# Attention scores of two heads in one product, over 128 rows with zeros beside the keys

## The chip, the core and the metric

The kernel runs on one core of a Trainium2 chip. The metric is device time in microseconds (us) of one execution; lower is better. The kernel before takes 1866.67 us, the median of 3 runs (1866.61 to 1867.35). The five engines of a core run their own lists of instructions in order and wait for each other by semaphores: TensorE (PE: products, with the weight loads shown apart as PEld), VectorE (DVE), ScalarE (ACT), GpSimd (POOL) and SyncE (SP, which here issues DMAs).

## The reference

Three layers follow each other: an attention with banded masks, a dense mixture of 8 experts, and a feed-forward layer with a squared ReLU. The change lies in the attention alone.

```python
# q, k, v: (4, 8, 576, 64) float32
scores = (1 / sqrt(64)) * q @ k.transpose(0, 1, 3, 2)
rel = pos[:, None] - pos[None, :]
mask_plain = (rel >= 0) & (rel < 32)                       # heads 0 to 3
mask_dil = (rel >= 0) & (rel < 128) & (rel % 4 == 0)       # heads 4 to 7
scores = where(masks, scores, -1e9)
attn = exp(scores - max(scores)); attn = attn / (sum(attn) + 1e-9)
x = (attn @ v), heads side by side: (2304, 512)
P = gate(x @ w_gate)                      # Sinkhorn: 8 rounds of row and column sums
y = sum over e of P[:, e] * (relu(x @ w1[e]) @ w2[e])      # w1: 8 x 512 x 1024
out = (relu(y @ w_in) ** 2) @ w_out                        # w_in: 512 x 2048
```

## The kernel before

**Staging.** The attention works first, in the first 85 us or so of the span. The experts and the last layer follow, in products of float32r operands split into a high and a low part; they fill the rest of the span and no line of them is touched.

**Groups and slots.** Queries are cut into blocks of 32 (`QB`). A block sees 64 keys (`KB`): its own 32 and the 32 before it. For the dilated heads the positions are sorted by their remainder by 4 outside the kernel, so that their mask is a band too. Six blocks (`GB`) of four heads make a group; 4 batches x 2 sorts of heads x 3 thirds of the sequence make 24 groups. The function `slot(i)` writes out by hand what each engine does in one step of the pipeline: the scores of group i (`att_scores`), the exponential and the norm of group i-1 (`softmax`), the product with the values of group i-4 (`att_pv`), the transposes of group i-3 (`att_tr`), and the copy of group i-5 to its place (`att_x`). `fill(i)` adds three products of the first expert in ten of the later slots, `gate(...)` the gate's products in a few, and `warm_up(4)` four products on zeros in slots 0 to 2. The order on each engine is that of the code.

**Scores (L439 to L464).** One product (L448) writes the masks of the whole group into a PSUM bank: its stationary operand `spread_q` (L89) repeats a 32 x 32 identity over four heads, its moving operand is a row of masks (0 or -1e30). Then 24 products (L452), one for each block and head, add the scores. The rows of the array are the 64 elements of a head: two heads lie one above the other, in rows 0 to 63 and 64 to 127, and two pairs of heads lie side by side in the tile. The four heads of a block write to four strips of 32 partitions. Each of these float32 products is two weight loads and two matmul instructions of 64 columns. VectorE takes the maximum (L462) and subtracts it (L463).

**Transposes and values.** Three transposes (L482) turn a group's weights; two ScalarE copies (L487) put their halves into `pts`, a tile with zeros in the other half. `att_pv` (L496) has 12 products, 128 rows x 64 columns of weights: the two blocks that one transpose holds are multiplied in one product, because the keys of each stand beside zeros.

**Loads.** `load_qk(i + 2)` and `load_v(i - 1)` are issued by SP in `feed(i)`. The queries and keys of a group are one DMA of 416 KB into one of three buffers (L426 and L427), which becomes free when the scores of the group three before it are done; the values are one of 384 KB (L434). Each DMA signals one of eight semaphores in turn (DMAHW0 to DMAHW7), and SP waits with a DMA until the one that used its semaphore last has landed.

**The start (L1079 to L1107).** Memsets clear the mask tile's unused rows and the zero halves. ScalarE loads the first masks, casts them (L437), and then asks for `ident`. SP asks for groups 0 and 1, a tile of weights (512 KB), group 2 and the other masks. Seven products on zeros (L1098) run on TensorE meanwhile.

Of the kernel before, what the change touches and what calls it, by code (L numbers as in the profile page):

```python
# [10 lines left out]
F32 = mybir.dt.float32  # L11
F32R = mybir.dt.float32r
# [17 lines left out]
KCOLS = QC + PAD  # L30
DIL = 4
KC = DM // 128
FB = 256
# [18 lines left out]
def tile_kernel(ctx: ExitStack, tc: tile.TileContext, a):  # L52
    nc = tc.nc
# [9 lines left out]
    xfp = att.enter_context(tc.tile_pool(name="xfp", bufs=1))  # L63
    qkv = att.enter_context(tc.tile_pool(name="qkv", bufs=2))
# [19 lines left out]
    every = slice(0, KC)  # L84

    ident = const.tile([128, 128], F32, name="ident")
    mask = xfp.tile([128, 4 * GB + 2, KB], F32R, name="mask")
    mask_raw = xfp.tile([QB, 4 * GB + 2, KB], F32, name="mask_raw")
    spread_q = mask[:, :2].rearrange("p g k -> p (g k)")  # L89
    p_zero = [xfp.tile([128, 2, GB // 2, 4, QB], F32, name=f"pts{k}") for k in range(2)]  # L90
    wg = xfp.tile([128, KC, 32], F32, name="wg")
    warm = xfp.tile([128, 128], F32, name="warm")

# [9 lines left out]
    bufs = {"s": 2, "xt": 2, "pt": 1, "mm": 3}  # L103
# [177 lines left out]
    def xb():  # L281
        return post[0].tile([128, 2 * T], F32, tag="xb", name="xb", bufs=2)
# [137 lines left out]
    NG = len(groups)  # L420
    q_t, k_t, v_t, e_t, pt_t, xt_t = {}, {}, {}, {}, {}, {}

    def load_qk(i):
        if i < NG:
            b, hg, m = groups[i]
            z = qkv.tile([128, 2 * (QC + KCOLS)], F32, tag="qk", name="qk", bufs=3)  # L426
            nc.sync.dma_start(z, a["qk"][b, hg, m])  # L427
            q_t[i], k_t[i] = (y.rearrange("p (r n) -> p r n", r=2) for y in (z[:, :2 * QC], z[:, 2 * QC:]))

    def load_v(i):  # L430
        if i < NG:
            b, hg, m = groups[i]
            v_t[i] = qkv.tile([128, GB // 2, 4 * D], F32, tag="v", name="v", bufs=4)
            nc.sync.dma_start(v_t[i], a["v"][b, hg, m])  # L434

    def round_mask(g0, g1):
        nc.scalar.copy(mask[:QB, g0:g1], mask_raw[:, g0:g1])  # L437

    def att_scores(i):  # L439
        _, hg, m = groups[i]  # L440
        qt, kt = q_t.pop(i), k_t.pop(i)
        ps = psum.tile([128, 512], F32, tag="s", name="s")[:, :GB * KB].rearrange("p (g k) -> p g k", g=GB)
        k = m + 1 if hg else 0
        if hg == 0 and m > 0:
            mk = mask[:, 4:5, :].to_broadcast([128, GB, KB])
        else:
            mk = mask[:, 2 + GB * k:2 + GB * k + GB, :]
        nc.tensor.matmul(ps, spread_q, mk, start=True, stop=False, skip_group_check=True)  # L448
# [28 lines left out]
    def att_tr(i):  # L477

        ex = e_t.pop(i).rearrange("p g k -> p (g k)")
        ps = bank("s" if i >= NG - 2 else "pt")[:, :GB * KB]  # L480
        for c in range(GB // 2):
            nc.tensor.transpose(ps[:, c * 128:(c + 1) * 128], ex[:, c * 128:(c + 1) * 128], ident)  # L482
        pt_t[i] = p_zero[i % 2]
        for half in range(2):
            keys = slice(KB * half, KB * half + KB)
            copy = nc.vector.tensor_copy if half and i >= NG - 3 else nc.scalar.copy
            copy(pt_t[i][keys, half].rearrange("p c h q -> p (c h q)"), ps[keys])  # L487

    def att_pv(i):
        vt, pt = v_t.pop(i), pt_t.pop(i)  # L490
        xt_t[i] = psum.tile([128, 512], F32, tag="xt", name="xt")[:, :2 * QC].rearrange("p (r w) -> p r w", r=2)
        halves = xt_t[i].rearrange("p r (h w) -> p r h w", h=2)
        for c in range(GB // 2):
            for head in range(4):
                pr, h = divmod(head, 2)
                nc.tensor.matmul(  # L496
                    halves[D * h:D * h + D, pr, :, c * QB:c * QB + QB],
                    vt[:, c, head * D:head * D + D],
                    pt[:, :, c, head],
                    start=True,  # L500
                    stop=True,
                )

    def att_parts(i):
# [6 lines left out]
        else:  # L511
            n, step = S // DIL, DIL
        parts, c = [], 0
# [564 lines left out]

    with tc.manual_schedule():  # L1079
        nc.vector.memset(warm, 0.0)  # L1080
        for eng, g in ((nc.vector, slice(0, GB + 2)), (nc.gpsimd, slice(GB + 2, None))):
            for rows in (slice(QB, 2 * QB), slice(2 * QB, 128)):
                eng.memset(mask[rows, g].bitcast(F32), 0.0)
# [10 lines left out]
        nc.sync.dma_start(mask_raw[:, GB + 2:], a["mask"][:, GB + 2:])  # L1094

        ps = psum.tile([128, 512], F32, tag="s", name="s")
        for k in range(NWARM):
# [8 lines left out]
        nc.vector.tensor_copy(wr, warm)  # L1106
        nc.vector.memset(xr.bitcast(F32), 0.0)  # L1107
        gates = []
        last_lo = [lambda: None]

# [77 lines left out]
        def feed(i):  # L1188
            if i:
                load_qk(i + 2)  # L1190
                load_v(i - 1)
            if parts:
                parts.pop(0)()
            if 1 <= i < 4:
                round_mask(GB * i + 2, GB * i + GB + 2)
# [187 lines left out]
        for i in range(len(steps) + 1):  # L1383
# [30 lines left out]
            if mixed(i - 1):  # L1414
                v = l2_mixed(i - 1)
# [39 lines left out]
            if i + 1 in first[1:]:  # L1455
                c = first[1:].index(i + 1)
# [11 lines left out]
            if i == TURN + 2:  # L1468
                y = two(xb()) + two(xb())
# [40 lines left out]
def _layout(x):  # L1510
    q, k, v = x["q"], x["k"], x["v"]

    def order(z):
        lo = z[:, :4]
        hi = z[:, 4:].reshape(B, 4, S // DIL, DIL, D).transpose(0, 1, 3, 2, 4).reshape(B, 4, S, D)
        return np.stack([lo, hi], axis=1)
# [1 line left out]
    qo, ko, vo = order(q), order(k), order(v)  # L1518

    def pairs(z):  # L1520
        return z.reshape(B, 2, 2, 2, S, D).transpose(0, 1, 3, 5, 2, 4)
# [4 lines left out]
    ks = np.stack([kz[..., m * QC:m * QC + KCOLS] for m in range(NM)], axis=2)  # L1526

    vp = np.concatenate([np.zeros((B, 2, 4, PAD, D), v.dtype), vo], axis=3)
    vt = np.stack([vp[:, :, :, j * QB:j * QB + KB] for j in range(NB)], axis=3)
    vt = vt.reshape(B, 2, 4, NM, 2, GB // 2, KB, D).transpose(0, 1, 3, 4, 6, 5, 2, 7)  # L1530
    vt = vt.reshape(B, 2, NM, 128, GB // 2, 4 * D)

    def first(w, n):
        return w.reshape(KC, 128, n, FC, 128).transpose(2, 1, 3, 0, 4).reshape(n, 128, KC * FB)
# [10 lines left out]
    def split_at(o):  # L1545
# [1 line left out]

    first_block, split, after_split = split_at(0), split_at(QB // 2), band & (kk >= QB // 2)
    masks = [
        z[3 * (k % 2) + k // 2]  # L1550
        for z in (
            [first_block] + [band] * 5,
            [first_block, band, band, band, split, after_split],
            [band, band, band, first_block, band, band],
            [band, split, after_split, band, band, band],
        )
        for k in range(GB)
    ]
    arrays = {
        "qk": np.concatenate([z.reshape(B, 2, NM, 128, -1) for z in (qs, ks)], axis=-1),  # L1560
        "v": vt,
        "w_gate": np.pad(x["moe_w_gate"].reshape(KC, 128, E).transpose(1, 0, 2), ((0, 0), (0, 0), (0, 32 - E))),
        "w1": w1,
# [1 line left out]
        "w_in": first(x["moe2_w_in"], NS2),  # L1565
        "w_out": second(x["moe2_w_out"], NS2),
        "mask": np.concatenate(
            [np.tile(np.eye(QB, dtype=np.float32), (1, 4)).reshape(QB, 2, KB)]
            + [np.where(m, 0.0, NEG).astype(np.float32)[:, None] for m in masks],
            axis=1,  # L1570
        ),
# [22 lines left out]
```

## Time and profile before

| | |
|---|---|
| median of 3 runs | 1866.67 us (1866.61 to 1867.35) |
| the profiled execution: its own time | 1866.62 us |
| its span | 1864.8 us |
| TensorE busy | 1852.2 us, 99% of the span |
| VectorE, ScalarE, GpSimd busy | 88%, 48%, 41% |
| DMA | 493.28 MB, 265 GB/s over the span |
[...]

The span runs from the first instruction to the last; 1.8 us of the own time lie around it. A matmul's busy time overlaps with that of the matmuls beside it in other strips of the array, so a busy share near 100% does not say that nothing could be shorter. "issue" as a releaser is time in which an engine waited for nothing that the profile shows.

### The profile page before, as it was taken

Reading aid. Unit: us, or ns where it says so; the run is one execution under the profiler, and the core shown is the slowest. Engines: PE = TensorE matmul, PEld = TensorE weight load, DVE = VectorE, ACT = ScalarE, POOL = GpSimd, SP = SyncE. Lnnn points to the kernel's source line nnn. Section 1 sums busy time; section 2 is a strip of 40 time slices with the busy share of each in tenths; the row PEclk is TensorE's granted clock in tenths of the full one; section 3 lists DMA queues with packets and bytes.
Section 4 is the critical chain, followed back from the end, with each engine's and each line's share of the span. In section 5 each row is a group of like instructions: output and inputs, shape, how many; then the busy total and the mean of one; then the engine's idle time right before and its main releaser. Section 6 shows DMA issues by size and latency. Waiting matters only on the chain.

```text
span 1864.8 us, 28269 instructions
## 1 busy us (share of the span) xinstructions
PE 1852.2 (99%) x10209; PEld 1541.8 (83%) x10209; DVE 1648.2 (88%) x2357; ACT 902.9 (48%) x1553; POOL 760.4 (41%) x650
## 2 busy tenths in 40 slices
PE   9999999999999999999999999999999999999999
PEld 7788888888888888888888888888888888888887
DVE  7788999999999999997799999999998879875775
ACT  6752444555554544543443444444343465653454
POOL 4532656556656555553323323232222443321321
PEclk9999999999999999999999999999999999999999
DMA  8785576667666665768887787777676798889562
GB/s 294 249 332 181 213 252 242 257 243 241 231 228 245 244 231 219 254 220 343 325 320 267 288 296 278 283 274 288 246 288 250 304 355 292 284 310 387 196 255 77
DMA packets 154684, 493.28 MB, mean 265 GB/s; under 512 B 16992, under 2 KB 20720, under 8 KB 154544
## 3 DMA queue, kind: packets, MB, share of 16 engines
q1 hardware_dynamic: 154208, 491.22, 71.7%
q8 instruction: 80, 1.31, 0.3%
q14 instruction: 60, 0.49, 0.1%
q10 hardware_dynamic: 336, 0.26, 0.1%
HBM read 282.67 MB, written 208.74 MB: 264 GB/s over the span
## 4 chain that ended last, share of the span: by engine, by line
PE 93%; DVE 4%; ACT 1%; issue 1%; POOL 0%; DMA 0%; SPq 0%; ACTq 0%; POOLq 0%; DVEq 0%
PE pt L646 17%; PE mm L1013 16%; PE s L1013 14%; PE s L646 11%; PE xt L646 11%; PE mm L904 10%; PE mm L840 5%; PE xt L1013 2%; PE mm L883 2%; DVE g L736 1%; PE xt L496 1%; PE s L452 1%; DVE acc L1024 1%; PE s L904 1%; PE mm L646 0%
## 5 line engine op out<-in xcount | busy, mean ns | idle before, releaser
L736 DVE TENSOR_TENSOR g<-r,g 128x512 fp32r<-128x512 f32 x268 | 306.3, 1155 | 37.0 <-ACT g L733 35.1
L766 POOL TENSOR_TENSOR r<-mix,r 128x512 f32<-128x512 f32 x67 | 87.4, 1304 | 568.8 <-DVE mix L754 494.3
L1013 PE MATMUL s<-g,mixh 128*128 128x512 f32 x670 | 207.2, 390 | 1.1 <-ACT mm L1035 0.4
L1013 PE MATMUL mm<-g,w2h 128*128 128x512 f32 x670 | 206.5, 390 | 0.7 <-ACT s L1035 0.7
L733 ACT CAST g<-r 128x512 fp32r<-128x512 f32 x268 | 166.0, 620 | 66.4 <-PE s L1013 34.3
L1024 DVE TENSOR_TENSOR acc<-mm,acc 128x512 f32<-128x512 f32 x266 | 180.5, 681 | 1.8 <-PE mm L1013 1.8
L1024 DVE TENSOR_TENSOR acc<-s,acc 128x512 f32<-128x512 f32 x260 | 171.9, 682 | 0.1
L736 DVE TENSOR_TENSOR g<-mix,g 128x512 fp32r<-128x512 f32 x201 | 158.7, 790 | 2.9 <-ACT g L733 2.9
L733 ACT CAST g<-mix 128x512 fp32r<-128x512 f32 x201 | 124.7, 621 | 72.2 <-DVE mix L754 45.1
L1013 PEld LDWEIGHTS s<-g,mixh 128*128 128x128 f32 x670 | 125.4, 188 | 29.3 <-ACT s L1035 1.7
L1013 PEld LDWEIGHTS mm<-g,w2h 128*128 128x128 f32 x670 | 125.6, 188 | 27.3 <-ACT s L1035 1.1
L250 POOL TENSOR_TENSOR raw<-raw 128x256 f32<-128x256 f32 x36 | 37.9, 1053 | 238.2 <-DVE w2l L178 214.5
L1013 PE MATMUL mm<-g,w2l 128*128 128x512 f32 x335 | 130.4, 389 | 0.0
L805 ACT COPY s<-pt 128x512 f32<-128x512 f32 x79 | 46.5, 588 | 165.3 <-PE pt L646 165.3
L764 POOL TENSOR_TENSOR mix<-mix,r 128x512 f32<-128x512 f32 x67 | 88.5, 1320 | 87.9 <-DVE g L736 87.9
L646 PE MATMUL xt<-x_hi,sumh 128*128 128x512 f32 x316 | 123.7, 391 | 0.1
L646 PE MATMUL s<-x_hi,blkh 128*128 128x512 f32 x316 | 123.5, 391 | 0.0
L646 PE MATMUL s<-x_lo,blkh 128*128 128x512 f32 x316 | 123.2, 390 | 0.0
L646 PE MATMUL pt<-x_hi,sumh 128*128 128x512 f32 x316 | 123.1, 390 | 0.0
L646 PE MATMUL xt<-x_lo,sumh 128*128 128x512 f32 x316 | 123.1, 390 | 0.0
L646 PE MATMUL xt<-x_hi,suml 128*128 128x512 f32 x316 | 123.1, 389 | 0.0
L646 PE MATMUL s<-x_hi,blkl 128*128 128x512 f32 x316 | 123.1, 389 | 0.0
(299 smaller groups left out, 5026.0 us busy)
## 6 DMA issues: line engine op xcount, KB each, us to landing
raw<-in_w SPq DMA_DIRECT2D x62, 512.0 KB, 4.2
w_blkh<-blkh SPq DMA_DIRECT2D x40, 512.0 KB, 5.1
w_blkl<-blkl SPq DMA_DIRECT2D x40, 512.0 KB, 5.9
w_sumh<-sumh SPq DMA_DIRECT2D x40, 512.0 KB, 6.2
w_suml<-suml SPq DMA_DIRECT2D x40, 512.0 KB, 4.7
w_w2h<-w2h SPq DMA_DIRECT2D x40, 512.0 KB, 5.6
w_w2l<-w2l SPq DMA_DIRECT2D x40, 512.0 KB, 5.7
blkh<-w_blkh SPq DMA_DIRECT2D x40, 512.0 KB, 3.8
```

The source lines that it names most:

```text
L250: tt(out=r[:, 1, 1], in0=r[:, 0, 1], in1=r[:, 1, 1], op=ALU.add)
L646: nc.tensor.matmul(ps, w[:, c], z[:, x, j], start=start and k == 0, stop=stop and k == 5, skip_group_check=True)
L733: after(k, lambda: nc.scalar.copy(b[:, 0], src))
L736: lambda: nc.vector.tensor_tensor(out=b[:, 1], in0=src, in1=b[:, 0].bitcast(F32), op=ALU.subtract),
L764: after(6 if i in (TURN, first[3]) else 4, lambda: nc.gpsimd.tensor_tensor(out=r3, in0=r3, in1=r5, op=ALU.subtract))
L766: sub = lambda o, x, y: nc.gpsimd.tensor_tensor(out=o, in0=x, in1=y, op=ALU.subtract)
L805: at_once(lambda: nc.scalar.copy(made["s2"], bank_b))
L840: nc.tensor.matmul(ps, w[:, c], z[:, kc], start=k == 0, stop=k == len(terms) - 1)
L883: nc.tensor.matmul(ps, wt, g, start=n == 0, stop=n == len(terms) - 1)
L904: nc.tensor.matmul(ps, g[:, c0 * 128:c0 * 128 + 128], wt[:, fc], start=k == 0 and not seeded, stop=k == 3 * FC - 1, skip_group_check=bool( ...
L1013: nc.tensor.matmul(ps, w[wt][:, c], block[n][:, g], start=start and k == 0, stop=stop and k == 2, skip_group_check=True)
L1024: nc.vector.tensor_tensor(out=o, in0=ps, in1=o, op=ALU.add)
```

## The change

A group's queries and keys come in two DMAs of 64 rows each (208 KB each) into one static tile `kq_all` with three places. In a place, keys stand twice: the first 448 columns hold keys in rows 0 to 63 and zeros below them, the last 448 hold zeros in rows 0 to 63 and keys below. Between them stand the 384 columns of queries, with one head in rows 0 to 63 and another in rows 64 to 127. One product has all 128 rows, 32 columns of queries and 128 moving columns, the 64 keys of the first head and the 64 of the second; 12 products make a group's scores. The four strips of partitions now hold two halves of the group's blocks by two pairs of heads. VectorE clears the zeros once, six memsets of 64 x 448 at the start. The values, the masks and the copies are laid out anew for this; a mask row is given once for two heads and repeated by the access pattern, and the stationary operand spreads two blocks' masks, so that the mask tile is 14 rows of 64 on 64 partitions, not 26 on 32. At the start ScalarE also issues the second half of group 0 and `ident` ahead of the mask's cast.

```diff
-            z = qkv.tile([128, 2 * (QC + KCOLS)], F32, tag="qk", name="qk", bufs=3)
-            nc.sync.dma_start(z, a["qk"][b, hg, m])
-            q_t[i], k_t[i] = (y.rearrange("p (r n) -> p r n", r=2) for y in (z[:, :2 * QC], z[:, 2 * QC:]))
+            z = kq_all[:, KQW * (i % 3):KQW * (i % 3) + 2 * (QW + KW)]
+            nc.sync.dma_start(z[:D, :KW + QW], a["kq"][b, hg, m, :D])
+            eng.dma_start(z[D:, KW:KQW], a["kq"][b, hg, m, D:])
+            k_t[i] = z.rearrange("p (h n) -> p h n", h=2)
+            q_t[i] = z[:, KW:KW + QW].rearrange("p (r n) -> p r n", r=2)
...
-        for g in range(GB):
-            for head in range(4):
-                pr, rows = head // 2, slice(D * (head % 2), D * (head % 2) + D)
+        for c in range(CB):
+            for quarter in range(4):
+                part, pr = divmod(quarter, 2)
+                n = QB * (CB * part + c)
                 nc.tensor.matmul(
-                    ps[QB * head:QB * head + QB, 2 * (g % 3) + g // 3, :],
-                    qt[rows, pr, g * QB:g * QB + QB],
-                    kt[rows, pr, g * QB:g * QB + KB],
+                    whole[QB * quarter:QB * quarter + QB, c],
+                    qt[:, pr, n:n + QB],
+                    kt[:, :, KCOLS * pr + n:KCOLS * pr + n + KB],
...
-        nc.scalar.dma_start(mask_raw[:, :GB + 2], a["mask"][:, :GB + 2])
-        round_mask(0, GB + 2)
+        nc.scalar.dma_start(mask_raw[:, :CB + 2], a["mask"][:, :CB + 2])
+        load_qk(0, nc.scalar)
         nc.scalar.dma_start(ident, a["ident"])
-        load_qk(0)
+        round_mask(0, CB + 2)
         load_qk(1)
...
+        for k in range(3):
+            z = kq_all[:, KQW * k:KQW * k + KQW]
+            nc.vector.memset(z[D:, :KW], 0.0)
+            nc.vector.memset(z[:D, KW + QW:], 0.0)
+            if k == 0:
+                nc.vector.tensor_copy(wr, warm)
+                nc.vector.memset(xr.bitcast(F32), 0.0)
```

On TensorE, in slots 6 and 7, the list of before reads as follows (`xt` is the product with the values, `pt` the transposes, `s` the bank of masks and scores; x24 counts products):

```order
L496 MATMUL xt<-pts_93,v 64x2x32 x12
L482 MATMUL pt<-ident,ms 128x128 x3
L448 MATMUL s<-mask 128x384
L452 MATMUL s<-qk 32x64 x24
L496 MATMUL xt<-pts_92,v 64x2x32 x12
L482 MATMUL pt<-ident,ms 128x128 x3
L448 MATMUL s<-mask 128x384
L452 MATMUL s<-qk 32x64 x24
```

The same place of the changed kernel, on TensorE:

```order
L506 MATMUL xt<-pts_93,v 64x2x32 x12
L492 MATMUL pt<-ident,ms 128x128 x3
L454 MATMUL s<-mask 128x384
L462 MATMUL s<-kq_all 32x128 x12
L506 MATMUL xt<-pts_92,v 64x2x32 x12
L492 MATMUL pt<-ident,ms 128x128 x3
L457 MATMUL s<-mask 128x384
L462 MATMUL s<-kq_all 32x128 x12
```

Nothing changes its place; a slot has 12 score products of 128 columns where it had 24 of 64, and the other products stay in number.

On SP, from the load of group 6 on, the list of before with its waits (PE is the wait for the buffer, DMAHW that for an earlier DMA on the same semaphore):

```order
L427 DMA qk<-in_qk 128x832 [waits DMAHW7_49,DMAHW6_49,PE_49]
L434 DMA v<-in_v 128x768
L427 DMA qk<-in_qk 128x832 [waits DMAHW1_49,DMAHW0_49,PE_49]
L434 DMA v<-in_v 128x768 [waits PE_49]
L427 DMA qk<-in_qk 128x832 [waits DMAHW3_49,DMAHW2_49,PE_49]
L434 DMA v<-in_v 128x768 [waits PE_49]
```

The same loads of the changed kernel, on SP:

```order
L432 DMA kq_all<-in_kq 64x832 [waits DMAHW4_49,PE_49]
L433 DMA kq_all<-in_kq 64x832 [waits DMAHW5_49]
L441 DMA v<-in_v 128x768 [waits DMAHW6_49]
L432 DMA kq_all<-in_kq 64x832 [waits DMAHW7_49,PE_49]
L433 DMA kq_all<-in_kq 64x832 [waits DMAHW0_49]
L441 DMA v<-in_v 128x768 [waits DMAHW1_49,PE_49]
L432 DMA kq_all<-in_kq 64x832 [waits DMAHW2_49,PE_49]
L433 DMA kq_all<-in_kq 64x832 [waits DMAHW3_49]
L441 DMA v<-in_v 128x768 [waits DMAHW4_49,PE_49]
```

A slot has three DMAs where it had two, each with a wait for the DMA eight before it, so the eight semaphores reach back two and two thirds slots where they reached back four. From the last slots of the attention to the end of the program the lists of all engines are the same in both kernels.

## Rows read from the trace of the kernel before

**Rows 1.** The page: TensorE's busy time, and the chain by line.

```profile
PE 1852.2 (99%) x10209; PEld 1541.8 (83%) x10209; DVE 1648.2 (88%) x2357; ACT 902.9 (48%) x1553; POOL 760.4 (41%) x650
...
PE pt L646 17%; PE mm L1013 16%; PE s L1013 14%; PE s L646 11%; PE xt L646 11%; PE mm L904 10%; PE mm L840 5%; PE xt L1013 2%; PE mm L883 2%; DVE g L736 1%; PE xt L496 1%; PE s L452 1%; DVE acc L1024 1%; PE s L904 1%; PE mm L646 0%
```

**Rows 2.** Stretches: from:to, length, busy by engine, clock, DMA share, GB/s.

```profile
15.40:33.90 18.50, 15.91 (x503) 12.93 (x504) 15.57 (x39) 14.95 (x34) 9.59 (x12) 1.00 0.96 329
33.90:56.30 22.40, 21.75 (x567) 16.20 (x567) 17.25 (x42) 17.87 (x44) 8.51 (x9) 1.00 0.88 290
```

**Rows 3.** The score products' line: duration in ns, min/median/max.

```profile
L452 PE MATMUL s<-qk x1152: 215/216/313, 5.5 to 75.3; 64*32 64x64 f32 x192
```

**Rows 4.** Timeline of TensorE, around 41.9 and 54.3 us: start, length.

```profile
41.84 0.26 PE L452 MATMUL s<-qk 64*32 64x64 f32 x4
...
41.84 0.87 PE L452 MATMUL s<-qk 64*32 64x64 f32 x48
...
54.11 0.64 PE L534 MATMUL s<-xf,wg 128*32 128x512 f32 x4
...
54.11 1.06 PE L534 MATMUL s<-xf,wg 128*32 128x512 f32 x8
```

**Rows 5.** Waits of the weight loads: us in total, times, longest.

```profile
PEld xt L496 <- ACT pts L487: 2.7, 9, 0.5
```

**Rows 6.** Timeline of TensorE, 17.1 to 34.2 us, in brackets idle before.

```profile
17.83 0.86 PE L452 MATMUL s<-qk 64*32 64x64 f32 x45
19.78 0.30 PE L452 MATMUL s<-qk 64*32 64x64 f32 x3 [1.09 <-issue]
...
24.02 0.52 PE L452 MATMUL s<-qk 64*32 64x64 f32 x19
24.70 0.64 PE L452 MATMUL s<-qk 64*32 64x64 f32 x29 [0.16 <-issue]
...
32.57 0.86 PE L452 MATMUL s<-qk 64*32 64x64 f32 x44
33.86 0.30 PE L452 MATMUL s<-qk 64*32 64x64 f32 x4 [0.42 <-issue]
```

**Rows 7.** DMA queues from 15.4 to 33.9 us: packets, MB, share.

```profile
q8 instruction: 4, 0.07, 1.4%
```

**Rows 8.** The chain in order of time, 17 to 35 us.

```profile
29.04 0.10 issue
...
33.43 0.42 issue
```

**Rows 9.** Timeline of ACT and DVE, 17.7 to 22.4 us.

```profile
17.77 0.97 ACT L487 COPY pts<-pt 64x384 f32<-64x384 f32 x2
...
20.11 0.56 DVE L462 TENSOR_REDUCE mx<-s 128x6 f32<-128x384 f32 x1 [1.30 <-PE s L452]
...
21.50 0.97 ACT L487 COPY pts<-pt 64x384 f32<-64x384 f32 x2 [1.33 <-PE pt L482]
```

**Rows 10.** The 24 loads of queries and keys: SP's issue (ns), us to landing.

```profile
L427 SPq DMA_DIRECT2D qk<-in_qk x24: 327/328/432, 0.7 to 65.4; - x24
...
DMA to landing us min/median/max: 3.2/4.4/6.3
```

**Rows 11.** Start: timeline; DMAs issued at 0.7 to 1.0 us, KB, us to landing.

```profile
2.59 0.48 DVE L1107 MEMSET xr<- 128x512 f32 x1
...
4.26 0.62 ACT L437 CAST mask<-mask_raw 32x512 fp32r<-32x512 f32 x1 [1.78 <-DMA mask_raw<-in_mask]
...
5.55 1.51 PE L452 MATMUL s<-qk 64*32 64x64 f32 x48
...
7.12 0.56 DVE L462 TENSOR_REDUCE mx<-s 128x6 f32<-128x384 f32 x1 [4.04 <-PE s L452]
...
qk<-in_qk SPq DMA_DIRECT2D x1, 416.0 KB, 4.0
mask_raw<-in_mask ACTq DMA_DIRECT2D x1, 64.0 KB, 3.5
```

More of the change, by code (lines that the diff above doesn't have):

```diff
@@ L30 @@
 KCOLS = QC + PAD
+CB = GB // 2
+QW = 2 * QC
+KW = 2 * KCOLS
+KQW = 2 * KW + QW
 DIL = 4
@@ L86, in tile_kernel @@
     ident = const.tile([128, 128], F32, name="ident")
[L87 to L90, printed above, removed]
+    mask = xfp.tile([128, 4 * CB + 2, 1, KB], F32R, name="mask")
+    mask_raw = xfp.tile([2 * QB, 4 * CB + 2, KB], F32, name="mask_raw")
+    spread_q = mask[:, :2].rearrange("p c h k -> p (c h k)")
+    p_zero = [xfp.tile([128, 2, CB, 4, QB], F32, name=f"pts{k}") for k in range(2)]
+    kq_all = xfp.tile([128, 3 * KQW + QW], F32, name="kq_all")
     wg = xfp.tile([128, KC, 32], F32, name="wg")
@@ L432, in load_v, with round_mask @@
             b, hg, m = groups[i]
-            v_t[i] = qkv.tile([128, GB // 2, 4 * D], F32, tag="v", name="v", bufs=4)
+            v_t[i] = qkv.tile([128, CB, 4 * D], F32, tag="v", name="v", bufs=4)
             nc.sync.dma_start(v_t[i], a["v"][b, hg, m])
-    def round_mask(g0, g1):
-        nc.scalar.copy(mask[:QB, g0:g1], mask_raw[:, g0:g1])
+    def round_mask(c0, c1):
+        nc.scalar.copy(mask[:2 * QB, c0:c1, 0], mask_raw[:, c0:c1])
     def att_scores(i):
@@ L443, in att_scores @@
         k = m + 1 if hg else 0
+        whole = ps.rearrange("p (c h) k -> p c h k", h=2)
         if hg == 0 and m > 0:
-            mk = mask[:, 4:5, :].to_broadcast([128, GB, KB])
-        else:
-            mk = mask[:, 2 + GB * k:2 + GB * k + GB, :]
-        nc.tensor.matmul(ps, spread_q, mk, start=True, stop=False, skip_group_check=True)
-        for g in range(GB):
-            for head in range(4):
-                pr, rows = head // 2, slice(D * (head % 2), D * (head % 2) + D)
+            mk = mask[:, 3, :, :].to_broadcast([128, GB, KB])
+            nc.tensor.matmul(ps, spread_q, mk, start=True, stop=False, skip_group_check=True)
+        else:
+            mk = mask[:, 2 + CB * k:2 + CB * k + CB].to_broadcast([128, CB, 2, KB])
+            nc.tensor.matmul(whole, spread_q, mk, start=True, stop=False, skip_group_check=True)
+        for c in range(CB):
+            for quarter in range(4):
+                part, pr = divmod(quarter, 2)
+                n = QB * (CB * part + c)
                 nc.tensor.matmul(
-                    ps[QB * head:QB * head + QB, 2 * (g % 3) + g // 3, :],
-                    qt[rows, pr, g * QB:g * QB + QB],
-                    kt[rows, pr, g * QB:g * QB + KB],
+                    whole[QB * quarter:QB * quarter + QB, c],
+                    qt[:, pr, n:n + QB],
+                    kt[:, :, KCOLS * pr + n:KCOLS * pr + n + KB],
                     start=False,
@@ L480, in att_tr @@
         ps = bank("s" if i >= NG - 2 else "pt")[:, :GB * KB]
-        for c in range(GB // 2):
+        for c in range(CB):
             nc.tensor.transpose(ps[:, c * 128:(c + 1) * 128], ex[:, c * 128:(c + 1) * 128], ident)
@@ L491, in att_pv @@
         xt_t[i] = psum.tile([128, 512], F32, tag="xt", name="xt")[:, :2 * QC].rearrange("p (r w) -> p r w", r=2)
[L492 to L495, printed above, removed]
+        for c in range(CB):
+            for quarter in range(4):
+                part, pr = divmod(quarter, 2)
+                n = QB * (CB * part + c)
                 nc.tensor.matmul(
-                    halves[D * h:D * h + D, pr, :, c * QB:c * QB + QB],
-                    vt[:, c, head * D:head * D + D],
-                    pt[:, :, c, head],
+                    xt_t[i][D * pr:D * pr + D, :, n:n + QB],
+                    vt[:, c, quarter * D:quarter * D + D],
+                    pt[:, :, c, quarter],
                     start=True,
@@ L1080, in tile_kernel @@
         nc.vector.memset(warm, 0.0)
-        for eng, g in ((nc.vector, slice(0, GB + 2)), (nc.gpsimd, slice(GB + 2, None))):
-            for rows in (slice(QB, 2 * QB), slice(2 * QB, 128)):
-                eng.memset(mask[rows, g].bitcast(F32), 0.0)
+        for eng, c in ((nc.vector, slice(0, CB + 2)), (nc.gpsimd, slice(CB + 2, None))):
+            eng.memset(mask[2 * QB:, c].bitcast(F32), 0.0)
         for z in p_zero:
@@ L1093, in tile_kernel @@
         load_qk(2)
-        nc.sync.dma_start(mask_raw[:, GB + 2:], a["mask"][:, GB + 2:])
+        nc.sync.dma_start(mask_raw[:, CB + 2:], a["mask"][:, CB + 2:])
         ps = psum.tile([128, 512], F32, tag="s", name="s")
@@ L1194, in feed @@
             if 1 <= i < 4:
-                round_mask(GB * i + 2, GB * i + GB + 2)
+                round_mask(CB * i + 2, CB * i + CB + 2)
             if i == 3:
@@ L1526, in _layout @@
     ks = np.stack([kz[..., m * QC:m * QC + KCOLS] for m in range(NM)], axis=2)
+    qs, ks = (z.reshape(B, 2, NM, 128, -1) for z in (qs, ks))
+    upper, lower = ((ks[:, :, :, :D], qs[:, :, :, :D]), (qs[:, :, :, D:], ks[:, :, :, D:]))
+    kq = np.concatenate([np.concatenate(z, axis=-1) for z in (upper, lower)], axis=3)
     vp = np.concatenate([np.zeros((B, 2, 4, PAD, D), v.dtype), vo], axis=3)
     vt = np.stack([vp[:, :, :, j * QB:j * QB + KB] for j in range(NB)], axis=3)
-    vt = vt.reshape(B, 2, 4, NM, 2, GB // 2, KB, D).transpose(0, 1, 3, 4, 6, 5, 2, 7)
-    vt = vt.reshape(B, 2, NM, 128, GB // 2, 4 * D)
+    vt = vt.reshape(B, 2, 2, 2, NM, 2, CB, KB, D).transpose(0, 1, 4, 2, 7, 6, 5, 3, 8)
+    vt = vt.reshape(B, 2, NM, 128, CB, 4 * D)
     def first(w, n):
@@ L1549, in _layout @@
     masks = [
-        z[3 * (k % 2) + k // 2]
+        np.concatenate([z[c], z[CB + c]])
         for z in (
@@ L1556, in _layout @@
         )
-        for k in range(GB)
+        for c in range(CB)
     ]
+    spread = np.kron(np.eye(2), np.tile(np.eye(QB), (1, 2))).astype(np.float32)
     arrays = {
-        "qk": np.concatenate([z.reshape(B, 2, NM, 128, -1) for z in (qs, ks)], axis=-1),
+        "kq": kq,
         "v": vt,
```

8 lines of the change are left out of this document (3 added, 5 removed).

## The prediction

> **What bounds the kernel now.** I read the page first, then its chain by line, then the attention's stretch by windows, the timeline of each engine in it, and last the waits around single instructions. TensorE is busy for 99% of the span, and of the lines that the change rewrites L452 and L496 have 1% of the chain each [rows 1]. So the change can move little: the scores' 24 slots of 0.87 us are 20.9 us [rows 4]. In the attention TensorE is not full. From 15.4 to 33.9 us it is busy for 15.91 of 18.50 us, in the next stretch it lacks 0.65 of 22.40 us [rows 2]. The 2.6 us missing in the first are what I looked at closely.
>
> **The score products.** Before, a slot has 24 products, each two matmul instructions (1152 in 24 slots [rows 3]). The 48 take 0.87 us, the last of them 0.216 [rows 3, 4], so one starts every (870 - 216) / 47 = 14 ns. A cut at 41.9 us shows why: four run at once [rows 4], one in each strip of 32 partitions; 12 rounds of four, of (870 - 216) / 11 = 59 ns for 64 columns. After, there are 24 instructions of 128 columns, with 128 rows and the same strips: 6 rounds of four. The trace has that form in the gate's products (L534), 128 rows by 32 columns. A cut at 54.3 us finds four of them at once too, and the second round of 512 columns ends 1.06 - 0.64 = 0.42 us after the first [rows 4]: 0.82 ns a column, 52.5 ns for 64 and 105 for 128. Each strip streams 12 x 64 = 768 columns before and 6 x 128 = 768 after. What goes is the fixed part of six rounds, 59 - 52.5 = 6.5 ns each, 0.04 us a slot; the first round's start is in it too, so I take 0.03. It counts where TensorE sets the pace; before L496 it waits for ScalarE's copies nine times anyway [rows 5]. So 15 x 0.03 = 0.45 us gained. The ends: nothing, and 24 x 0.04 = 0.96 us.
>
> [...] The trace shows four at once before, since each head has a strip of its own, so the halves that stood empty are what the zeros now fill.
>
> **Stalls within the products.** In slot 5 TensorE stops after 45 of 48 score instructions and goes on 1.09 us later, with "issue" as the reason [rows 6]. It stops again after 19 at 24.5, at 29.04, and after 44 at 33.4 us [rows 6, 8]. A slot has 48 instructions for scores, 24 for values, 3 transposes and 1 for the mask, 76 with a weight load each. From the first stop to the second there are 3 + 28 + 48 + 28 + 19 = 126, from the second to the last 29 + 28 + 48 + 28 + 48 + 28 + 44 = 253, twice that, with the one at 29.04 between. So TensorE stops every 126 pairs of a load and a matmul, and in just this stretch the DMA's instruction queue brings four packets, 0.07 MB [rows 7]. I read the stops as waits for the next block of TensorE's instructions: it uses one up in 126 / 76 = 1.7 slots, while DMA is 96% busy [rows 2].
>
> After the change a slot has 24 + 28 = 52 pairs, and a block lasts 126 / 52 = 2.4 slots. From 17.83 to 32.57 us are five slots [rows 6]; without the stops that is 2.6 us a slot, so a block lasts 6.3 us and not 4.4. Is each stop on the path? At the first, ScalarE's copies, for which the values' products wait, end at 17.77 + 0.97 = 18.74 us, when the scores would be done too; then VectorE waits 1.30 and ScalarE 1.33 us for TensorE [rows 9]. All 1.09 count. The second stands before a wait for ScalarE and counts nothing. The other two are links of the chain themselves, 0.10 and 0.42 [rows 8]. Together 1.61 us. A block that has 1.9 us more should come in time, except perhaps once at the busiest; I take 1.3 us gained. Ends: nothing (the stops only move) and 1.6 us.
>
> [...]
>
> **Loads.** The bytes stay; a slot's two DMAs become three, 0.33 to 0.43 us of SP each [rows 10], at most 1.3 of 2.6 us. Queued behind the second half's issue is the load of the values, which slips by as much; its products come three slots later. But without the first stop the scores of group 6 come a microsecond sooner, in the stretch where DMA is fullest, and loads take up to 6.3 us [rows 10]. I charge 0.3 us for a late landing or two; ends 0 and 1 us. The new wait for the DMA eight before reaches back 8 / 3 = 2.67 slots, 7.0 us, against 4.4 us to landing in the median [rows 10]: nothing in the forecast, a rival below.
>
> **The start.** The mask's load decides when TensorE starts: it lands 3.5 us after its issue, the cast follows, then the mask's product and the scores at 5.55 us [rows 11]. It grows from 64 to 80 KB in 64 rows. The cast shrinks from 512 to 320 elements a row: by the elements from 0.62 to 0.39 us. Group 0's second half now stands behind the mask on ScalarE's queue, beside group 1's first half, and `ident` comes early: up to 288 KB more may be ahead of its last byte. At 329 GB/s [rows 2] that is 0.9 us later than 0.7 + 4.0, 5.6 us, where the first score product started at 5.55. I take +0.15 us; ends -0.2 and +0.5. The six memsets of 448 columns last 0.48 x 448 / 512 = 0.42 us each, 2.5 us on VectorE, less 0.66 for one mask memset of 320 columns in place of two of 512. VectorE, free at 2.59 + 0.48 us before, is free near 5 us, inside its 4.04 us of waiting for the first scores at 7.12 [rows 11]; without that cover they cost 1.9 us. The later, shorter mask casts lie beside products on zeros: nothing.
>
> **Sum.** -0.45 - 1.3 + 0.3 + 0.15 = -1.3 us. The profiled execution's own 1866.62 us (span 1864.8 and 1.8 around it) become 1865.3; it lies 0.05 under the median of the runs, so I forecast 1865.4 us. After the attention the lists are the same and TensorE is full, so the gain should stay. The ends add up to -0.96 - 1.6 - 0.2 = -2.8 and 1 + 0.5 = +1.5: 1863.9 to 1868.2.
>
> **Rivals.**
> - *The stops move and nothing is gained.* Blocks end elsewhere after the change, and each may stop TensorE anew while DMA is 96% busy; or ScalarE, busy for 14.95 of 18.50 us [rows 2], takes the time back. For it: the blocks come over the same DMA as the loads. Against it: from 36 to 75 us, in slots with more work for each pair, no product stops in its middle. That leaves -0.45 + 0.45: 1866.7 us.
> - *Loads bound the attention, and the kernel is slower.* Three DMAs a slot on eight semaphores: if landing takes longer than 2.67 slots, SP stands, and a slot stretches to landing / 2.67. It decides from 7.0 us. At 7.8 us a slot is 2.9; over 20 slots +6 us, less the 1.3: 1871. For it: 6.3 us has been seen [rows 10]. Against it: the median of 4.4, and no wait of TensorE for a load before.
> - *Time goes by the count of instructions.* Were the 14 ns a price per instruction and not of columns, 24 would take half: -0.33 us a slot, -5 in the 15 slots that count, -8 in all, and the stops: 1857 to 1860. For it: the rows of L452 alone can't tell the two apart. Against it: a round of L534 goes by its columns [rows 4]. [...]
> - *Products of 128 rows don't run four at once.* 24 x 0.105 = 2.5 us a slot, +1.9, over 24 slots +45: 1911 us. Against it: four of L534 at once [rows 4].
>
> **How the numbers follow.** What a measurement of this kernel can tell from no change is 0.2%, 3.7 us. The forecast has 0.72 (its own range 1863.9 to 1866.4), nothing gained 0.14, loads 0.08, count 0.03, no concurrency 0.02, something unseen 0.01. Faster by over 0.2% takes the count rival or what is unseen or undercounted: 0.05. Slower takes half of the loads rival, the last rival and the unseen: 0.07. Within 0.2%: 0.88. The range, 1863.4 to 1868.2, holds the ends of the sum, the first rival and the mild part of the second.
>
> **What would show it.** Right: 576 score instructions, 24 in about 0.85 us, each near 270 ns, four at once; the stops of 1.09 and 0.42 us gone or under 0.3; the first score product within 0.3 us of 5.55; the attention's end 1 to 2 us earlier. Wrong: SP standing at DMA semaphores, scores that wait for loads, stops every 126 pairs as long as before, or a gain that appears only after the attention.

## The result, and the profile of the changed kernel

The changed kernel takes **1877.67 us**, the median of 6 runs (1874.30 to 1883.51), against 1866.90 us (1866.54 to 1867.36) for the kernel before in the same session: a ratio of 1.0061 with a 95% interval of 1.0042 to 1.0080. It is slower by some 11 us, where 1865.4 and a range to 1868.2 were forecast. The profiled execution took 1877.62 us, its span is 1875.8 us; TensorE's granted clock is 1.00 in the attention, as before. Why the six runs of the changed kernel lie 9 us apart was not found.

The page of the changed kernel, TensorE's busy time and the chain by line:

```profile
PE 1850.8 (99%) x9633; PEld 1537.2 (82%) x9633; DVE 1650.8 (88%) x2362; ACT 903.0 (48%) x1553; POOL 757.3 (40%) x649
...
PE pt L656 17%; PE mm L1023 16%; PE s L1023 14%; PE s L656 11%; PE xt L656 11%; PE mm L914 10%; PE mm L850 5%; DMA kq_all<-in_kq 4%; PE xt L1023 2%; PE mm L893 2%; DVE g L746 1%; DVE acc L1034 1%; PE s L914 1%; PE s L462 0%; DMA raw<-w 0%
```

Against [rows 1] one name is new: the DMA of queries and keys is 4% of the chain, where no DMA had as much as 0.5%. The same stretches as [rows 2], and the next one:

```profile
15.40:33.90 18.50, 13.68 (x309) 10.95 (x310) 13.12 (x34) 12.62 (x28) 8.82 (x10) 1.00 1.04 283
33.90:56.30 22.40, 19.41 (x380) 14.50 (x382) 16.41 (x41) 16.67 (x42) 6.83 (x7) 1.00 1.05 243
56.30:76.00 19.70, 15.96 (x288) 11.75 (x284) 13.56 (x33) 13.59 (x29) 11.95 (x10) 1.00 1.05 238
```

Every engine does less in the same time. DMA's share has gone from 0.96 and 0.88 to above 1 (it sums the times of all packets, so it can pass 1), while DMA moves less: 283 and 243 GB/s for 329 and 290. The line of the score products in the changed kernel, with what ended TensorE's idle time before them:

```profile
L462 PE MATMUL s<-kq_all x576: 269/273/421, 5.3 to 84.5; 128*32 128x128 f32 x192
...
  DMA kq_all<-in_kq: 30.4, 31
```

The products are as forecast (576 of 273 ns); what is new is that they wait for their load 31 times (products and weight loads are counted apart, so the same wait can stand twice). TensorE's timeline, slots 5 to 9, answers to [rows 6]:

```profile
19.96 0.86 PE L462 MATMUL s<-kq_all 128*32 128x128 f32 x24 [1.96 <-DMA kq_all<-in_kq]
...
23.25 0.86 PE L462 MATMUL s<-kq_all 128*32 128x128 f32 x24 [0.92 <-DMA kq_all<-in_kq]
...
26.08 0.86 PE L462 MATMUL s<-kq_all 128*32 128x128 f32 x24 [0.46 <-DMA kq_all<-in_kq]
...
29.15 0.98 PE L462 MATMUL s<-kq_all 128*32 128x128 f32 x24 [0.70 <-DMA kq_all<-in_kq]
...
32.15 0.86 PE L462 MATMUL s<-kq_all 128*32 128x128 f32 x24 [0.53 <-DMA kq_all<-in_kq]
```

No stop stands inside a group's 24 products any more; a wait for the load stands before each. A slot is (32.15 - 19.96) / 4 = 3.05 us, where it was (32.57 - 17.83) / 5 = 2.95 with the stops [rows 6]. DMA from 15.4 to 33.9 us of the changed kernel (queue: packets, MB, share of the 16 engines; then loads, KB each, median us to landing):

```profile
q1 hardware_dynamic: 2050, 5.20, 103.6%
...
kq_all<-in_kq SPq DMA_DIRECT2D x12, 208.0 KB, 7.2
v<-in_v SPq DMA_DIRECT2D x6, 384.0 KB, 7.8
```

The same row of the kernel before:

```profile
q1 hardware_dynamic: 2238, 6.02, 94.5%
```

I divide the bytes by the busy time of all 16 engines: 6.02 MB / (0.945 x 18.5 us) = 344 GB/s before, 5.20 / (1.036 x 18.5) = 271 after. So it is not that more is asked of DMA: the same bytes take it longer. The loads land after 7.2 us (median of the stretch) where [rows 10] has 4.4 (4.5 in the same stretch). SP stands at DMA semaphores in the changed kernel (0 to 80 us; total, times, longest):

```profile
SPq L441 <- DMA v<-in_v: 5.7, 4, 1.5
SPq L432 <- DMA v<-in_v: 4.7, 4, 2.3
SPq L432 <- DMA kq_all<-in_kq: 2.7, 7, 0.5
SPq L433 <- DMA kq_all<-in_kq: 2.3, 7, 0.6
```

The first products behind the attention (L850, L840 before) start at 97.8 us; the same row of before says 88.6:

```profile
L850 PE MATMUL xt<-xs,blkh x16: 278/281/387, 97.8 to 101.7; 128*128 128x256 f32 x16
```

```profile
L840 PE MATMUL xt<-xs,blkh x16: 278/281/387, 88.6 to 92.5; 128*128 128x256 f32 x16
```

9.2 of the 11.0 us between the spans are there at the attention's end. The remaining 1.8 us come in small pieces over the rest; their cause was not found. Most of the loss comes after the stretch shown: the scores of slot 10 start 2.5 us later than before (35.02 against 32.57 us), the last score product of all 9.2 us later (84.5 against 75.3 [rows 3]).

### The profile page after: what moved, and what is told of

The parts are those of the page before. It is cut to its first block, busy times and chain, and to the rows that moved or that the text cites. A ratio compares the mean times of both kernels' runs of the same rounds, so it can differ in the third digit from the quotient of the medians.

```text
span 1875.8 us, 27172 instructions
## 1 busy us (share of the span) xinstructions
PE 1850.8 (99%) x9633; PEld 1537.2 (82%) x9633; DVE 1650.8 (88%) x2362; ACT 903.0 (48%) x1553; POOL 757.3 (40%) x649
## 4 chain that ended last, share of the span: by engine, by line
PE 90%; DMA 4%; DVE 4%; ACT 1%; issue 1%; SPq 0%; POOL 0%; ACTq 0%; POOLq 0%; DVEq 0%
PE pt L656 17%; PE mm L1023 16%; PE s L1023 14%; PE s L656 11%; PE xt L656 11%; PE mm L914 10%; PE mm L850 5%; DMA kq_all<-in_kq 4%; PE xt L1023 2%; PE mm L893 2%; DVE g L746 1%; DVE acc L1034 1%; PE s L914 1%; PE s L462 0%; DMA raw<-w 0%
```

## The experiments

Three theories. **A:** a transfer into 64 neighbouring rows is slow for DMA itself. **B:** the number counts: three DMAs a slot on eight semaphores, the rival of the prediction. **C:** the products with zeros, or something else of the change, cost the time. All times are medians; ratios are to the kernel before on the same chip.

| kernel | us (runs) | ratio, 95% interval | GB/s while busy, 15.4 to 33.9 us |
|---|---|---|---|
| before, two DMAs of 64 neighbouring rows | 1879.16 (4) | 1.0069 [1.0054, 1.0084] | 4.84 / (1.020 x 18.5) = 256 |
| before, two DMAs of half the columns | 1865.85 (10) | 1.0000 [0.9990, 1.0009] | 5.78 / (0.915 x 18.5) = 341 |
| before, two DMAs, even and odd rows | 1867.47 (10) | 1.0009 [0.9999, 1.0018] | 5.01 / (0.831 x 18.5) = 326 |
| changed, heads on even and odd rows | 1864.60 (10) | 0.9996 [0.9986, 1.0005] | 5.95 / (0.930 x 18.5) = 346 |
| the same again | 1863.66 (11) | 0.9989 [0.9980, 0.9998] | |
| changed, even and odd, other start | 1863.83 (11) | 0.9988 [0.9979, 0.9997] | |
| changed, rows 64 to 127 on ScalarE's queue | 1886.94 (4) | 1.0115 [1.0101, 1.0129] | |
| before, three DMAs of 32, 64, 32 rows | 1873.11 (4) | 1.0039 [1.0025, 1.0053] | 5.18 / (0.977 x 18.5) = 287 |

**The kernel before with its load in two halves of the rows.** Products, zeros and places stay as before.

```diff
-            nc.sync.dma_start(z, a["qk"][b, hg, m])
+            for h in (slice(0, D), slice(D, 128)):
+                nc.sync.dma_start(z[h], a["qk"][b, hg, m, h])
```

> The kernel before, with one edit: the load of queries and keys is two DMAs of 64 neighbouring rows (0 to 63, 64 to 127). Theory A (a transfer that writes only 64 neighbouring rows moves slower, whatever the products do): the attention is as slow as in the changed kernel, 1874 to 1883 us, TensorE waits for loads in most slots, loads land after 7 us or more. Theory B (three DMAs a slot on eight semaphores hold SP back): also 1874 to 1883 us. Theory C (the products of 128 rows or their zeros cost the time): 1866.9 us as before.

It loses 13 us, all that the change loses and more. The waits of its weight loads, 0 to 110 us, and DMA from 15.4 to 33.9 us:

```profile
PEld s L453 <- DMA qk<-in_qk: 9.3, 14, 1.6
```

```profile
q1 hardware_dynamic: 1917, 4.84, 102.0%
...
qk<-in_qk SPq DMA_DIRECT2D x12, 208.0 KB, 7.6
```

Not all of the 13 us is the loads themselves. In the profiled execution, the fastest of the four (1877.48 us), TensorE's granted clock is 0.51 from 51.3 to 54.7 us; it fell within a stop of 2.36 us. By these two numbers I estimate that TensorE can have lost up to 0.49 x 3.4 = 1.7 us there. The other three have lower mean clocks still, 0.996 and 0.997. The changed kernel's profiled execution loses its 11 us without such a stretch. So C falls: the loads, with what follows from them, do it. A and B both allow it; the next two tell them apart.

**The same with two halves of the columns,** in all 128 rows each: as many DMAs, as many semaphores.

```diff
-            nc.sync.dma_start(z, a["qk"][b, hg, m])
+            for h in (slice(0, QC + KCOLS), slice(QC + KCOLS, None)):
+                nc.sync.dma_start(z[:, h], a["qk"][b, hg, m, :, h])
```

> The kernel before, with the load of queries and keys as two DMAs of all 128 rows, half of the columns each: as many DMAs, bytes and waits as with two halves of the rows. Theory A (rows): 1866 to 1868 us, no wait of TensorE for a load. Theory B (number of DMAs): 1874 to 1883 us. Theory C (products): 1866.9 us.

No time is lost, and the loads land after 4.2 us in the median of 48. The products wait for them twice, 1.3 us in all, where no wait was expected. B falls.

**The same with even and odd rows:** 64 rows a DMA again, every second row.

```diff
-            nc.sync.dma_start(z, a["qk"][b, hg, m])
+            for h in range(2):
+                nc.sync.dma_start(z[h::2], a["qk"][b, hg, m, D * h:D * h + D])
```

> The kernel before, with the load as two DMAs of 64 rows each, one on the even and one on the odd rows: same number, rows and bytes as two neighbouring halves, only spread over the whole tile. Theory A: 1866 to 1868 us, loads land after 4 to 5 us. Theory B: 1874 to 1883 us. If it is the count of 64 rows and not their place that makes a transfer slow: 1874 to 1883 us.

64 rows as such are not slow: 326 GB/s while busy, 4.7 us to landing, and a time within 0.2% of before. (Its profiled execution is the slowest of the ten, 1869.35 us; from 21.9 to 25.2 us the granted clock is 0.50.) It is where they lie.

**The changed kernel with its two heads on even and odd rows.** The zeros then lie in every second row, so VectorE and GpSimd clear the keys' columns over all rows before the loads.

```diff
-            nc.sync.dma_start(z[:D, :KW + QW], a["kq"][b, hg, m, :D])
-            eng.dma_start(z[D:, KW:KQW], a["kq"][b, hg, m, D:])
+            nc.sync.dma_start(z[0::2, :KW + QW], a["kq"][b, hg, m, :D])
+            eng.dma_start(z[1::2, KW:KQW], a["kq"][b, hg, m, D:])
```

> The changed kernel, with the two heads of a product on the even and the odd rows, not on the lower and the upper half; the key columns are cleared over all rows before the first loads, which starts the attention about 1 us later. Theory A: the 11 us come back; 1866 to 1867 us: the forecast gain of 1.3 us less the later start; scores 24 in 0.85 us, stops of TensorE for its instructions under 0.3 us. Theory B and theory C: 1874 to 1884 us.

All the loss is gone, and a little of the forecast gain appears: 1864.60 us, and 1863.66 when run again beside the next one. The first products behind the attention start at 86.5 us, and at 85.7 the second time, where before has 88.6. The score products' line of this kernel, and DMA from 15.4 to 33.9 us:

```profile
L462 PE MATMUL s<-kq_all x576: 269/273/421, 5.1 to 73.0; 128*32 128x128 f32 x192
...
  DMA kq_all<-in_kq: 3.3, 7
```

```profile
q1 hardware_dynamic: 2327, 5.95, 93.0%
...
kq_all<-in_kq SPq DMA_DIRECT2D x16, 208.0 KB, 4.9
```

It has three DMAs a slot on the same eight semaphores, and 3.3 us of waits where the changed kernel has 30.4.

> The changed kernel with the heads on even and odd rows again, beside the new order of the start, for a closer comparison of the two: 1864.6 us as before by both theories, and packets of 131 ns.

**Both halves in flight at once?** ScalarE's queue issues the second half, rows 64 to 127.

```diff
-            eng.dma_start(z[D:, KW:KQW], a["kq"][b, hg, m, D:])
+            (nc.scalar if i > 2 else eng).dma_start(z[D:, KW:KQW], a["kq"][b, hg, m, D:])
```

> The changed kernel, but ScalarE's queue issues the second half (rows 64 to 127) of every group from the fourth on, so that both halves of a group can be in flight at the same time. Theory D: transfers into rows 0 to 63 and into rows 64 to 127 hold each other up only because one follows the other in one queue, and every DMA engine is on the same half of the rows at a time. Then two queues bring the packets of 3328 bytes from 200-231 ns back to about 131, 15 to 34 us moves 320 GB/s and not 283, and TensorE's waits for kq_all (34 us in the 31 waits listed, weight loads included) go; the issues cost ScalarE some 0.55 us a slot, which makes it the bound in places: 1866 to 1872 us. Theory E: a transfer of 64 neighbouring rows is slow whatever stands beside it. Then packets stay above 190 ns, and the time stays at 1876 to 1882 us, with ScalarE's issues on top.

Slower than either theory said, for a reason that I had left out. ScalarE's timeline:

```profile
23.47 0.47 ACT L497 COPY pts<-pt 64x384 f32<-64x384 f32 x1 [4.80 <-PE pt L492]
23.48 0.47 ACTq L433 DMA_DIRECT2D kq_all<-in_kq  x1
```

The issue stands in ScalarE's list behind work that waits for TensorE (4.80 us here), and TensorE waits for the load. Three times TensorE's granted clock falls to 0.50 for 3.4 us, the first time at 19.7 us after a wait of 3.26 us; by my estimate, 3 x 0.50 x 3.4, that can hold up to 5 of the 21 us lost. DMA has gaps (0.90 busy from 15 to 34 us), and both halves are in flight together only in part of the time, so this is no clean test of D and E. But D's forecast does not come out: from 15.4 to 33.9 us the packets of 3328 bytes last 186 ns in the median on SP's queue and 180 on ScalarE's, not 131, and the rate while busy is 4.39 / (0.897 x 18.5) = 264 GB/s, no more than with both halves on one queue (271).

**Where do the 64 rows have to lie?** The kernel before, with rows 32 to 95 in one DMA and 32 rows on either side.

```diff
-            nc.sync.dma_start(z, a["qk"][b, hg, m])
+            for h in (slice(0, 32), slice(32, 96), slice(96, 128)):
+                nc.sync.dma_start(z[h], a["qk"][b, hg, m, h])
```

> The kernel before, but the load of queries and keys in three DMAs of neighbouring rows: 0 to 31, 32 to 95, 96 to 127. Theory F: what counts is which half of the 128 rows a DMA writes, so that 64 neighbouring rows across the middle are as quick as 128. Then the packets of the middle DMA take about 131 ns and those of the two others about 200 or more, and the time lies between before and the two halves: 1867 to 1875 us. Theory G: 64 or fewer neighbouring rows are slow wherever they lie. Then all packets take about 200 ns and the time is 1877 us or more, as with two halves. If the number of DMAs were what costs: four a slot, 1880 us or more with packets of 131 ns.

7 us lost where the two halves lose 13: the time lies in Theory F's range. It does not show F, though. In the profiled execution the products wait for these loads for 2.0 us in 2 places (with the two halves 6.4 us in 10), and TensorE has two stretches at a lower clock:

```profile
13.20:16.60 3.40, 3.40 (x54) 2.49 (x53) 1.82 (x6) 1.34 (x3) 0.83 (x1) 0.50 1.01 297
23.40:26.80 3.40, 3.40 (x70) 2.78 (x68) 2.40 (x6) 1.85 (x4) 1.78 (x2) 0.50 1.00 287
```

The clock of 0.50 follows on a wait of 1.80 us for a load and on a stop of 2.05 us with "issue"; busy throughout, TensorE can have lost up to 0.50 x 3.40 = 1.7 us in each stretch, an estimate. The four runs go by it: 1870.35 us at a mean clock of 1.000, 1872.74 at 0.999, 1873.49 at 0.998, 1874.88 at 0.997. At most some 4 us are left for the place of the rows. Nor are the packets Theory F's: by their records from 15.4 to 33.9 us they are not of two kinds, and last 176 ns in the median (131 before, 202 with two halves). Transfers of both kinds are in flight together, so this can't tell which is held up by which. The two probes below can.

**Another order at the start** of the even and odd kernel, for a faster version:

```diff
-        nc.scalar.dma_start(ident, a["ident"])
+        load_qk(1, nc.scalar)
         round_mask(0, CB + 2)
-        load_qk(1)
-        nc.sync.dma_start(raw1.rearrange("p b c -> p (b c)"), src_w(0, 0))
         load_qk(2)
         nc.sync.dma_start(mask_raw[:, CB + 2:], a["mask"][:, CB + 2:])
+        nc.sync.dma_start(ident, a["ident"])
+        nc.sync.dma_start(raw1.rearrange("p b c -> p (b c)"), src_w(0, 0))
```

> The changed kernel with the heads on even and odd rows and another order at the start: ScalarE issues the second half of groups 0 and 1, SP the first halves, then group 2, the other masks, ident, and last the 512 KB of weights, which are first read at 17 us; GpSimd and VectorE change places in clearing the zeros. With even and odd rows alone TensorE waited 1.27 us at 7.5 and 1.00 us at 11.0 us for the loads of groups 1 and 2, which landed at 8.7 and 11.9 us behind the weights. Theory H: the start is on the path and both waits go: 2 us less than with even and odd rows alone (1864.6), 1862.6 us, faster than both kernels. Rival: DMA is 93% busy to 34 us, the weights only land later, and TensorE waits for other loads or for ScalarE instead: 1864 to 1865 us.

The rival holds: 1863.83 us against 1863.66. The third group's scores start at 10.27 us (11.24 without the new order), but then TensorE waits at later loads instead:

```profile
14.18 0.86 PE L462 MATMUL s<-kq_all 128*32 128x128 f32 x24 [0.30 <-DMA kq_all<-in_kq]
...
16.88 0.86 PE L462 MATMUL s<-kq_all 128*32 128x128 f32 x24 [0.33 <-DMA kq_all<-in_kq]
```

**Single transfers behind the kernel's end,** nothing else in DMA, each waiting for the one before:

```diff
+            nc.sync.dma_start(dst[:64], src[:64])
...
+            nc.sync.dma_start(dst[32:96], src[32:96])
...
+            nc.sync.dma_start(dst[0::2], src[:64])
```

> The changed kernel with single transfers behind its end, where no other DMA runs: packets of 3328 bytes from in_kq into a tile that is no longer used, each transfer waiting for the one before (a small one of 256-byte packets between them), in two rounds: all 128 rows; rows 0 to 63; 64 to 127; 32 to 95; the 64 even rows; both halves one after the other on one queue; both halves on two queues; even and odd rows one after the other. The whole time is longer by the probes and says nothing. Theory E (neighbouring rows of one half are slow by themselves, the half decides): 131 ns a packet for 128 rows and for even rows, 200 ns or more, up to twice 131, for rows 0 to 63 and for 64 to 127, 131 for rows 32 to 95; two halves on two queues between 131 and 200. Theory G (64 neighbouring rows are slow wherever they lie): 200 or more for rows 32 to 95 too. Rival (packets are slow only when transfers of several shapes overlap in the queue): 131 ns for each single transfer, whatever its rows.

By their packets the rival is right: 131 ns in the median for each shape that goes alone. Only the landing differs. Rows 0 to 63, then rows 32 to 95:

```profile
L1532 SPq DMA_DIRECT2D raw<-in_kq x2: 487/508/528, 1884.7 to 1924.6; - x2
...
DMA to landing us min/median/max: 3.1/3.1/3.1
```

```profile
L1536 SPq DMA_DIRECT2D raw<-in_kq x2: 536/546/556, 1894.3 to 1934.2; - x2
...
DMA to landing us min/median/max: 2.8/2.8/2.8
```

Rows 64 to 127 need 3.0 to 3.1 us, even rows 2.7 to 2.8, and all 128 rows, twice the bytes, 2.9 to 3.0. A single transfer's packets do not show where they are written; why not stays open. The two halves as a pair land some 3.8 us after the first issue whether one queue has both or two queues have one each; even and odd rows on one queue need 3.3. Hence streams:

```diff
+            for k in range(8):
+                b, hg, m = groups[k]
+                src = a["kq"][b, hg, m][D * (k % 2):D * (k % 2) + D]
+                engines[k % 2].dma_start(spaces[k][pair[k % 2]], src)
```

> The changed kernel with streams of transfers behind its end, where no other DMA runs: eight transfers in a row without a wait between them, packets of 3328 bytes, into eight places that are no longer used; between the streams one of eight transfers of all 128 rows, for comparison. Each stream twice. The whole time is longer by the probes and says nothing. A single transfer showed 131 ns a packet whatever its rows; only its landing was 0.3 to 0.4 us later for rows 0 to 63 or 64 to 127 (3.05 to 3.12 us) than for rows 32 to 95 or the even ones (2.68 to 2.85). Theory E (the half decides, and shows once transfers follow each other): all 128 rows 131 ns and 330 GB/s or more; rows 0 to 63 eight times 200 to 260 ns and half the rate, 165 to 210 GB/s; rows 32 to 95 and the even rows 131 ns and above 300 GB/s; the halves in turn on one queue between the two, 230 to 280 GB/s as in the changed kernel; on two queues as on one, or, if both halves are then written at the same time, 300 or more; even and odd in turn 131 ns and 300 or more. Rival (nothing in the rows, only the mixture with the loads of values): 131 ns and one rate for all.

Stretches from the middle of the streams (from:to, length, five idle engines, clock, DMA share, GB/s), in this order: rows 0 to 63, all rows, rows 32 to 95, even rows, both halves in turn, even and odd in turn:

```profile
1893.00:1898.00 5.00, 0.00 (x0) 0.00 (x0) 0.00 (x0) 0.00 (x0) 0.00 (x0) 0.50 1.04 208
1905.00:1910.00 5.00, 0.00 (x0) 0.00 (x0) 0.00 (x0) 0.00 (x0) 0.00 (x0) 0.50 0.98 334
1917.00:1921.00 4.00, 0.00 (x0) 0.00 (x0) 0.00 (x0) 0.00 (x0) 0.00 (x0) 0.50 0.90 286
1940.50:1944.50 4.00, 0.00 (x0) 0.00 (x0) 0.00 (x0) 0.00 (x0) 0.00 (x0) 0.50 0.95 291
1964.50:1969.50 5.00, 0.00 (x0) 0.00 (x0) 0.00 (x0) 0.00 (x0) 0.00 (x0) 0.50 1.00 262
...
2012.50:2016.50 4.00, 0.00 (x0) 0.00 (x0) 0.00 (x0) 0.00 (x0) 0.00 (x0) 0.50 0.91 295
```

Theory E stands in the form that it has here (the half decides) as far as the streams show it, for rows 0 to 63, and G falls: 64 neighbouring rows across the middle are as quick as every second row, and rows 0 to 63 are slow. (The quick ones stay short of the 300 GB/s that I expected.) The packets' records say the same: 265 ns in the median of that first stretch, twice 131; 131 for all rows, rows 32 to 95, even rows, and even and odd; 207 for the halves in turn. The second time round the six rates are 211, 318, 280, 287, 256 and 291. What keeps the quick shapes at 280 to 295, under the 318 to 334 of all rows, is open: SP issues one of 208 KB every 0.63 us, which would allow 338 GB/s, and their share is 0.86 to 0.95. Rows 64 to 127 were not streamed by themselves on one queue. The stream on two queues is no test: ScalarE's four transfers ran first, SP's after them. Whether both halves at once would go at full rate is not shown; the pair on two queues above, and the run with ScalarE's queue, gave no sign of it.

## Why the prediction was wrong

- **Loads: the step that failed.** "The bytes stay" holds, and that they take the same time was taken for granted; the term had 0.3 us, ends 0 and 1. Measured alone it is +13 us in the kernel before, part of it, by the estimate above, by the lower clock (+11 in the run with one such stretch). Between the changed kernel and the even and odd one, each against before in its own session, it is 10.8 + 1.4 = 12 us and, the second time, 10.8 + 2.4 = 13, with a granted clock of 1.00 in all three profiled executions. I had looked at the landing times, the queue's semaphores and SP's issues, never at which rows a DMA writes. The rates of the streams give nearly the slot that came: 416 KB at 262 GB/s are 1.63 us, 384 KB at 334 are 1.18, together 2.8 us; 3.05 were measured from 20 to 32 us, where the values' packets are slower too (171 ns in the median, 121 before). Why rows 0 to 63 are slower to write than rows on both sides of the middle, no run shows. The warning stood in [rows 2]: at a share of 0.96, a rate that falls by a fifth is at once the bound.
- **The new DMA wait** was costed at nothing, with the loads rival deciding from 7.0 us to landing. Landing did pass it (median 7.4 us over the 24 first halves), SP did stand at DMA semaphores, and the slot of 3.05 us is 10% above 7.4 / 2.67 = 2.77. But the rival gave no reason for late landings, and the number of DMAs is not the reason: slow transfers are. With three DMAs a slot and quick transfers TensorE still waits for loads, but for 1.3 us in two places (half the columns), 2.3 in two (even and odd rows in the kernel before) and 2.6 in four (in the changed kernel), where the changed kernel has 15.6 in 19. Its 1871 us was also too little, and its 0.08 too small a chance.
- **Products: right,** but for the size. 24 take 0.86 us, where 0.84 were forecast, so 0.01 us a slot is gained and not 0.03; each lasts 273 ns, near 270. They start in fours, by the trace every 56 ns before and every 109 after, where 59 and 105 were reckoned. The cut at 41.9 us could not show four at once, since it stands at the start of a group: at 42.2 us it finds 15. The starts in fours bear the reading out. The rival of the instruction count and the one without concurrency fall by the same row.
- **Stops: right as far as seen.** In the changed kernel one stop of 0.15 us stands inside a group of products (at 35.8 us), in the even and odd one none, and in neither does a product wait with "issue" as the reason; the kernel before with even and odd rows still has them (1.93 and 1.05 us with "issue" before the last 6 and 10 instructions). DMA's instruction queue brings 15 packets from 5 to 84 us before, and 9 and 11 in the changed and in the even and odd kernel. That the stops are waits for these blocks is still argued from counts, not shown by a run of its own.
- **Start:** the first score product starts at 5.27 us, 0.28 earlier, where 0.15 later was forecast; that is 0.08 outside the ends of -0.2 and +0.5. The memsets stayed hidden.
- **The sum without the loads term** is -0.45 - 1.3 + 0.15 = -1.6 us. The even and odd kernel, which has the products and not the slow loads, differs from before by 1864.60 - 1866.03 = -1.4 and, the second time, by 1863.66 - 1866.09 = -2.4 us. So the rest of the working was sound to within what can be measured here (the first interval includes no change at all); how the gain divides between products and stops was not tested.

## What to carry to other kernels

Of each DMA that a change splits or moves, ask which rows it writes, not only how many bytes: rows 0 to 63 go at 208 GB/s, while 64 rows taken as every second row, or across the middle, go at 280 to 295 and keep the quick packets (131 ns). Where a layout needs two halves (two heads, two batches), interleave them by row: a sum over rows is the same in any order, the 24 products took 0.86 us either way, and here it turned a loss of 11 us into a gain of 1 to 2, which is hardly clear of the noise. And where DMA's share is already 0.96, bound each load's term by a rate that is a fifth lower (344 to 271 GB/s here) before it is called nothing. Where a wait grows, read the granted clock too: in three kernels that lost time it fell to 0.50 or 0.51, which can have been up to 1.7, 3.4 and 5 us of the loss by the estimates above.

## What the runs showed of the chip that I had not expected

A slow destination does not show in a single transfer: 131 ns a packet for rows 0 to 63 alone, 261 to 265 once eight follow each other. A profile of one load would have said that nothing is wrong but 0.3 us at its landing. The two halves in turn are quicker (262 GB/s, 207 ns) than rows 0 to 63 eight times (208), yet other loads beside them are slow too: in the changed kernel the packets of the values, which fill all 128 rows, take 167, 207 and 212 ns in the median of the three stretches where they took 121 before.
